# Three of the four inputs of a linear attention are transposed by transfers instead of by TensorE

## The chip, the cores and the metric
The kernel runs on one core of a Trainium2 chip. A core has engines with instruction queues of their own, each executed in order: TensorE (PE, with its weight loads PEld), VectorE (DVE), ScalarE (ACT), GpSimd (POOL) and SyncE (SP), which here only issues transfers. They wait for one another through semaphores. The metric is the device time of one execution in microseconds; three runs of the kernel before had a median of 473.02 us (472.58 to 473.94).

## The reference, cut to what matters
Sizes: 4 batches, 8 heads, 768 steps, head width 48; model width 384, hidden width 1536; all float32 (the weights of the MLP arrive as 64-bit floats).

```
f = sigmoid(f_logit)
for t in range(768):                                   # per batch and head
    state = f[t][:, None] * state + outer(k[t], v[t])  # 48 x 48
    y[t] = q[t] @ state
x = y, heads side by side                              # (4, 768, 384)
out = x + relu(layernorm(x) * g_ln @ w_ch1) @ w_ch2
```

## The kernel before, in words
The 768 steps are cut into twelve units of 64 steps, each with all batches and heads. For each unit n there are the stages of `attention(n)` and then `mlp(n)`, a generator whose `yield`s cut it into pieces.

The attention needs f, q and k with the head width on the partitions. They arrive with the steps on the partitions: a raw tile [128, 2, 8, 64] for each (two batches' 64 steps on the partitions, then two groups g, eight heads of 48 padded to 64). `across` (L607) turns one group with four 128x128 transposes on TensorE (L611) into a PSUM bank, so f, k and q take eight each for a unit. From PSUM, `do_gates` (L641) writes the sigmoids of f into a gate tile on ScalarE; `do_k` and `do_q` multiply k and q by running products of gates (kh, qh; L638, VectorE). The running products are scans on VectorE over a whole unit: `after` (L619) backwards, `upto` (L631) forwards. `kept` is the state multiplied by a unit's total gate. `do_carried` and `do_scores` are 64-row products on TensorE (py L689, ps L703), `do_causal` masks the scores (sc, L707), `do_values` multiplies them by v into py (L729) and copies x out on ScalarE, `do_kt` turns kh (kp L719, copied by L721), `do_chunk` and `do_state` make the next state. Then `normalize` and `turn` make xt (xp L792, scaled by L794), and `sums_of_x` makes sums of its blocks (y, L814).

From the fourth unit on (`FIRST`), the MLP has 15 products by blocks (`by_blocks`, L844, banks bw, bx, by, bz, bv), whose results are copied, added and put through a ReLU into h on ScalarE and VectorE; `sums` (s1 to s4, L823 to L826) on VectorE; then seven products p1, p2, p6, p5, p7, p3, p4 (pp, L935) whose results are added on VectorE and POOL and stored by SP (`put`, L948). PSUM has eight banks: two tiles of two banks (`two_banks`, for py, ps and pn in turn) and four of one bank (`one_bank`), taken in turn by everything else.

The order of every engine's work is written by hand in two strings. START has units 0 to 2 and the loading and unpacking of the weights; UNIT is formatted for each m from 3 to 11, with n = m + 1, o = m + 2, p = m + 3, z = m + 4. A token is one step, issued in this order on the queues of the engines that it uses: `a{n}.stage` a stage, `m{m}` the next piece of the MLP, `l{p}k` a load (four transfers from SP), `s{m}` and `y{n}` the sums, and in START `f`, `r`, `w` for a weight piece, `d` a filler product on TensorE, `t`, `T`, `u`, `U` for sums of weights on VectorE or POOL. Dependencies and buffers then become semaphore waits. A tile with a tag and `bufs=2` has two buffers taken in turn: a third user waits until the first one's readers are done.

Of the kernel before, what the change touches and what calls it, by code (L numbers as in the profile page):

```python
# [8 lines left out]
FP32 = mybir.dt.float32  # L9
I32 = mybir.dt.int32  # L10
U32 = mybir.dt.uint32
AF = mybir.ActivationFunctionType
ALU = mybir.AluOpType
PSUM = bass.MemoryType.PSUM
# [288 lines left out]


START = """
l0k f l0q a0.gates l0x a0.after l0v f r a0.kx a0.upto l1f
d a0.kept a0.k d l1x d d a0.q l1k a0.carried d a0.scores
d a0.causal a0.values w d r a0.kt a0.stats f l1q d a1.gates
f l1v a0.chunk d w a0.norm a1.after a0.state a0.turn d a1.upto a1.kx
a1.k d f r w m0 a1.kept m0 a1.q f f r  # L310
w a1.carried a1.kt r f r l2k f a1.scores a1.causal f l2v
w l2f f a1.values r a1.chunk f a1.stats m0 m0 r w
a1.norm m0 a1.turn r w r w a1.state m0 m1 m1 m1
w m1 w a2.gates r m0 m1 m0 a2.after r l2x w
l2q w a2.kx a2.k a2.upto m1 m0 a2.q m0 m0 l3q l3k
a2.kept l3v m0 a2.carried a2.scores U m1 a2.causal a2.values m1 a2.stats a2.norm
m1 m1 U l3f a2.kt U m1 a2.turn m1 a3.gates T a2.chunk
m2 a3.after a2.state a3.kx l3x l4f m2 a3.k a3.upto a3.kept m2 a3.q
U m2 U l4q a3.carried a3.scores a3.kt U U a3.causal U l4x
a4.gates l4k a3.values T l4v U U a3.chunk m2 a3.stats a3.state t  # L320
l5v U a3.norm m2 s2 a4.after m2 l5f a3.turn m2 m2 a4.kx
a4.k a4.upto l5x l5k m2 U u m2 a4.q m2 y3 l5q
a5.gates a4.kt m2 l6f a4.kept
"""
UNIT = """
m{m} m{m} m{m} a{n}.carried a{o}.after a{n}.scores a{n}.causal m{m} m{m} a{n}.values m{m} m{m}
m{m} m{m} a{n}.stats m{m} m{m} m{m} a{n}.norm m{m} m{m} m{m} s{m} a{n}.chunk
m{m} a{n}.turn m{m} a{o}.upto a{p}.gates a{o}.kx l{p}v a{o}.k a{n}.state m{m} m{m} m{m}
a{o}.kt y{n} m{m} a{o}.q l{p}q l{p}x a{o}.kept l{p}k m{m} l{z}f
"""  # L330


# [1 line left out]
def kernel(  # L334
# [19 lines left out]
    nc = tc.nc  # L354
    B, H, S, D = q.shape
    P = 128
    T = 64
    G = B // 2
    NP = H // 2
    GA = G * NP  # L360
    NS = 2 * GA
    E1 = T + 1
# [4 lines left out]
    NU = S // T  # L367
# [2 lines left out]
    LEAST = 1e-12  # L370
    PLAIN = 2
    FIRST = 3
    PIECE = 768

    outer = ctx.enter_context(tc.tile_pool(name="outer", bufs=1))
# [6 lines left out]
    fast = ExitStack()  # L382
# [2 lines left out]
    raws = fast.enter_context(tc.tile_pool(name="raws", bufs=2))  # L385
    work = fast.enter_context(tc.tile_pool(name="work", bufs=1))
    xs = fast.enter_context(tc.tile_pool(name="xs", bufs=3))
    ps2 = fast.enter_context(tc.tile_pool(name="ps2", bufs=2, space=PSUM))
    ps1 = fast.enter_context(tc.tile_pool(name="ps1", bufs=4, space=PSUM))

    changing = ExitStack()
    stage = changing.enter_context(tc.tile_pool(name="stage", bufs=2))

    def two_banks(name):
        return ps2.tile([P, 2, 512], FP32, tag="two", name=name)

    def one_bank(name):
        return ps1.tile([P, 512], FP32, tag="one", name=name)
# [5 lines left out]
    for name, fill in (("f", 40.0), ("q", 0.0), ("k", 0.0)):  # L404
        t = consts.tile([P, G, H, 64], FP32, name=f"{name}raw")
        nc.gpsimd.memset(t[:, :, :, D:64], fill)
        wide_heads[name] = t
    loaded = {}

    def load(n, name, engines=(nc.sync,)):  # L410
        if n >= NU:
            return
        if name == "x":

            loaded[n, name] = raws.tile([P, G, NP, D], FP32, tag="rawx", name=f"vx{n}")
            odd = v.rearrange("b (a r) s d -> b r s a d", r=2)
            for b in range(B):
                nc.sync.dma_start(out=loaded[n, name][(1 - b % 2) * T:(2 - b % 2) * T, b // 2],
                                  in_=odd[b, 1, n * T:(n + 1) * T])
            return  # L420
        if name == "v":
            vt = raws.tile([P, G, H, D], FP32, tag="rawv", name=f"v{n}")
            loaded[n, name] = vt
        else:
            loaded[n, name] = wide_heads[name]
        src = {"f": f_logit, "k": k, "q": q, "v": v}[name]
        for b in range(B):
            engines[b % len(engines)].dma_start(  # L428
                out=loaded[n, name][(b % 2) * T:(b % 2 + 1) * T, b // 2, :, 0:D],
                in_=src[b, :, n * T:(n + 1) * T, :].rearrange("h p d -> p h d"))  # L430
# [21 lines left out]
    nc.vector.memset(ends[:, :, T:E1], 1.0)  # L452
    starts = consts.tile([P, NS, E1], FP32)
    nc.vector.memset(starts, 0.0)
    gates = []
    for i in range(2):
        t = consts.tile([P, NS * E1 + 1], FP32, name=f"gates{i}")
        nc.gpsimd.memset(t, 0.0)
        gates.append(t)
    least = consts.tile([P, NS], FP32)  # L460
    nc.vector.memset(least, 1.0)
    state = consts.tile([P, 2, GA, D], FP32)
# [66 lines left out]
    mixed = [consts.tile([P, KH, CH], FP32, name=f"mixed{i}") for i in range(1, 5)]  # L529
    to_mix = list(range(0, KH, 2))  # L530

    nothing = consts.tile([P, P], FP32)
    nc.vector.memset(nothing, 0.0)

    def idle():

        nc.tensor.matmul(one_bank("idle")[:, 0:2 * P], lhsT=nothing,
                         rhs=nothing.unsqueeze(1).broadcast_to([P, 2, P]), start=True, stop=True)

    def mix(engine=nc.vector):  # L540
        rows = slice(to_mix[0], to_mix.pop(0) + 2)
# [52 lines left out]

    def attention(n):

        gt = gates[n % 2]
        gv = gt[:, 0:NS * E1].rearrange("p (s e) -> p s e", e=E1)
        HS = NS // G
        flat = "p s e -> p (s e)"  # L600
# [2 lines left out]
        def new(name, shape, **kw):  # L603
            at[name] = work.tile(shape, FP32, tag=name, name=f"{name}{n}", **kw)
            return at[name]
# [35 lines left out]
        def do_gates():  # L641
            new("after", [P, NS, E1])
            new("upto", [P, NS, E1])
            new("total", [P, NS], bufs=2)
            for g in range(G):
                segs = slice(g * HS, (g + 1) * HS)
                pt = across(loaded[n, "f"], g)
                nc.scalar.activation(out=gv[:, segs, 1:E1], in_=pt, func=AF.Sigmoid)  # L648
                if n == 0:
                    scan_after(segs)  # L650
                    scan_upto(segs)
# [7 lines left out]
                scan_upto(slice(0, NS))  # L659

        def do_k_across():
            at["pk"] = [across(loaded[n, "k"], g) for g in range(G)]

        def do_k():
            times(new("kh", [P, NS, T]), at["pk"], at["after"])

        def do_q():
            times(new("qh", [P, NS, T]), [across(loaded[n, "q"], g) for g in range(G)],
                  at["upto"])
            nc.vector.tensor_tensor(out=least, in0=least, in1=at["total"], op=ALU.min)  # L670

        def do_kept():
# [6 lines left out]

        def do_carried():  # L680

            at["py"] = py = two_banks(f"py{n}")
            if not n:
                return
            qh, kept = at["qh"], at["kept"]
            for e in range(GA):
                for b in range(2):
                    for r in range(2):
                        nc.tensor.matmul(py[half(b), r, e * D:(e + 1) * D],  # L689
                                         lhsT=qh[head_rows(r), 2 * e + b],  # L690
                                         rhs=kept[head_rows(r), b, e], start=e == 0, stop=False,
                                         skip_group_check=True)
# [286 lines left out]

    running = {}

    def run(plan):
        for token in plan.split():
            kind, rest = token[0], token[1:]
            if kind == "a":
                n, stage = rest.split(".")
                if int(n) >= NU:
                    continue  # L990
                if "a" + n not in running:
                    running["a" + n] = attention(int(n))
                running["a" + n].pop(stage)()
            elif kind == "m":
                if token not in running:
                    running[token] = mlp(int(rest))
                next(running[token])
            elif kind == "l":
                load(int(rest[:-1]), rest[-1])
            elif kind == "s":  # L1000
                sums(int(rest))
            elif kind == "y":
                if FIRST <= int(rest) < NU:
                    sums_of_x(int(rest))
            else:
                {"r": read, "w": write, "f": fetch, "t": mix, "d": idle,
                 "T": lambda: mix(nc.gpsimd), "u": mix_step,
                 "U": lambda: mix_step(nc.gpsimd)}[token]()
# [2 lines left out]
    assert not (queue or fetched or opened)  # L1011
    for m in range(3, NU):
        run(UNIT.format(m=m, n=m + 1, o=m + 2, p=m + 3, z=m + 4))
        if m == NU - 2:
            worst = consts.tile([P, 1], FP32)
            nc.vector.tensor_reduce(out=worst, in_=least, axis=mybir.AxisListType.X, op=ALU.min)
            pw = one_bank("pw")
            nc.tensor.transpose(pw[0:1, 0:P], worst, ident)
            least_one = consts.tile([1, 1], FP32)
            nc.vector.tensor_reduce(out=least_one, in_=pw[0:1, 0:P], axis=mybir.AxisListType.X,  # L1020
                                    op=ALU.min)
            nc.vector.tensor_scalar(out=small, in0=least_one, scalar1=LEAST, scalar2=None,
                                    op0=ALU.is_lt)
# [37 lines left out]
```

## Time and profile before

| | |
|---|---|
| median of three runs | 473.02 us |
| the profiled execution | 472.82 us, of which the span is 470.7 us |
| TensorE busy | 452.5 us, 96% |
| VectorE, ScalarE, POOL busy | 332.3, 149.7, 93.9 us |
| transfers | 36.32 MB; almost all from SP's queue, whose packets take 36.3% of 16 engines' span |

Busy time is the union of an engine's instructions. TensorE's instructions overlap, so the duration of one is longer than what it adds; what it adds is seen in the spacing of a row of them. The chain that ended last is followed back from the last instruction, at each step to what released it, or to the instruction before it on its engine. Line numbers are those of the kernel before.

### The profile page before, as it was taken

What the parts mean: (1) busy time and instruction counts of PE and PEld (TensorE: products, weight loads), DVE (VectorE), ACT (ScalarE), POOL (GpSimd) and SP (SyncE); (2) the same over time, 40 slices, a digit from 0 to 9 for tenths busy, and PEclk for the clock granted to TensorE, in tenths of its full rate; (3) what the DMA queues carried; (4) which work ended last, traced back from release to release, by engine and by line L of the source; (5) the groups of instructions that cost most, each with busy time, mean ns of one, the idle gap of its engine ahead of it and who ended that gap; (6) DMA issues with size and microseconds to landing.
All of it is one profiled execution on the core that took longest, in us unless ns stands there. A gap on an engine that the chain in (4) does not pass through costs nothing.

```text
span 470.7 us, 13070 instructions
## 1 busy us (share of the span) xinstructions
PE 452.5 (96%) x5655; PEld 420.3 (89%) x5655; DVE 332.3 (71%) x543; ACT 149.7 (32%) x298; POOL 93.9 (20%) x110
## 2 busy tenths in 40 slices
PE   5698999999999999999999999999999999999994
PEld 4487887668899999999999999999999999999994
DVE  6798978236698688578678678677768768666361
ACT  3256652013321341341251242243142241241320
POOL 3215534079222011011011011002002002002010
PEclk9989999999999999999999999999999999999998
DMA  9899980623463302512522522422422410100001
GB/s 167 163 215 239 262 218 2 135 45 65 81 117 78 76 3 55 99 35 52 96 43 52 101 37 50 87 54 43 92 54 42 78 36 9 29 1 18 17 10 33
DMA packets 125969, 36.32 MB, mean 77 GB/s; under 512 B 116432, under 2 KB 122064, under 8 KB 125904
## 3 DMA queue, kind: packets, MB, share of 16 engines
q1 hardware_dynamic: 124128, 35.02, 36.3%
q8 instruction: 46, 0.75, 0.7%
q10 hardware_dynamic: 1776, 0.40, 0.4%
q14 instruction: 19, 0.16, 0.1%
HBM read 30.67 MB, written 4.72 MB: 75 GB/s over the span
## 4 chain that ended last, share of the span: by engine, by line
PE 90%; DVE 3%; SPq 3%; DMA 1%; issue 0%; ACT 0%
PE pp L935 29%; PE bx L844 11%; PE ph L906 9%; PE by L844 9%; PE po L916 7%; PE tr L611 6%; PE bz L844 3%; PE py L729 3%; PE py L689 3%; PE ps L703 2%; PE pn L759 2%; PE kp L719 2%; SPq L428 2%; PE bv L844 2%; PE bw L844 2%; PE xp L792 2%
## 5 line engine op out<-in xcount | busy, mean ns | idle before, releaser
L906 PE MATMUL ph<-xt,w 128*128 128x256 f32 x216 | 48.6, 381 | 0.5 <-DVE kh L638 0.5
L906 PEld LDWEIGHTS ph<-xt,w 128*128 128x128 f32 x216 | 40.4, 190 | 6.5 <-issue 0.9
L935 PE MATMUL pp<-w,h 128*128 128x192 f32 x240 | 42.9, 329 | 0.0
L935 PE MATMUL pp<-mixed,h 128*128 128x192 f32 x240 | 42.3, 326 | 0.0
L935 PE MATMUL pp<-mixed,s 128*128 128x192 f32 x240 | 40.9, 326 | 0.0
L855 ACT ACTIVATE h<-h 128x512 f32<-128x512 f32 x45 | 28.3, 630 | 38.5 <-DVE h L852 37.2
L935 PEld LDWEIGHTS pp<-mixed,h 128*128 128x128 f32 x240 | 39.1, 190 | 0.0
L935 PEld LDWEIGHTS pp<-mixed,s 128*128 128x128 f32 x240 | 38.9, 190 | 0.1
L935 PEld LDWEIGHTS pp<-w,h 128*128 128x128 f32 x240 | 38.6, 190 | 0.4
L747 POOL TENSOR_SCALAR rstd<-mv 128x2 f32<-128x2 f32 x12 | 2.8, 235 | 180.8 <-DVE mv L746 180.7
L852 DVE TENSOR_TENSOR h<-h,by 128x512 f32<-128x512 f32 x36 | 24.8, 688 | 16.9 <-PE by L844 15.9
L619 DVE TENSOR_TENSOR_SCAN after<-gates,ends 128x1040 f32<-128x1040 f32 (+1 forms) x13 | 28.8, 2213 | 5.8 <-ACT gates L648 5.8
L916 PE MATMUL po<-w,h 128*128 128x384 f32 x96 | 32.5, 488 | 0.0
L721 ACT COPY kt<-kp 128x512 f32<-128x512 f32 x24 | 12.9, 591 | 57.5 <-PE kp L719 57.5
L707 DVE TENSOR_TENSOR sc<-ps,causal 128x1024 f32<-128x1024 f32 x12 | 14.7, 1225 | 22.9 <-PE ps L703 22.9
L631 DVE TENSOR_TENSOR_SCAN upto<-gates,starts 128x1040 f32<-128x1040 f32 (+1 forms) x13 | 29.7, 2282 | 0.5
L852 DVE TENSOR_TENSOR h<-h,bx 128x512 f32<-128x512 f32 x27 | 18.3, 679 | 15.9 <-PE bx L844 15.9
L844 PE MATMUL bx<-y,v 128*128 128x128 f32 x216 | 29.4, 279 | 0.0
L736 ACT COPY x<-py 128x384 f32<-128x384 f32 x24 | 10.3, 483 | 59.0 <-PE py L729 59.0
L916 PEld LDWEIGHTS po<-w,h 128*128 128x128 f32 x96 | 17.8, 190 | 10.8
L844 PEld LDWEIGHTS bx<-y,v 128*128 128x128 f32 x216 | 26.2, 192 | 0.7
L943 POOL TENSOR_TENSOR p1x<-p,x 128x192 f32<-128x192 f32 x10 | 10.3, 1032 | 70.9 <-ACT p L950 70.9
(153 smaller groups left out, 940.0 us busy)
## 6 DMA issues: line engine op xcount, KB each, us to landing
w_0words<-in_moe_w_ch_dram SPq DMA_DIRECT2D x7, 768.0 KB, 5.6
kraw<-in_k_dram SPq DMA_DIRECT2D x48, 96.0 KB, 3.4
qraw<-in_q_dram SPq DMA_DIRECT2D x48, 96.0 KB, 3.0
v<-in_v_dram SPq DMA_DIRECT2D x48, 96.0 KB, 3.0
fraw<-in_f_logit_dram SPq DMA_DIRECT2D x46, 96.0 KB, 3.0
vx<-in_v_dram SPq DMA_DIRECT2D x48, 48.0 KB, 2.8
out_dram<-p1x SPq DMA_DIRECT2D x19, 48.0 KB, 2.0
out_dram<-u4y SPq DMA_DIRECT2D x19, 48.0 KB, 2.0
```

What stands on the lines that cost most here:

```text
L611: nc.tensor.transpose(pt[:, a * P:(a + 1) * P], src[:, g, 2 * a:2 * a + 2].rearrange("p h e -> p (h e)"), ident)
L619: nc.vector.tensor_tensor_scan(out=at["after"].rearrange(flat)[:, c0:c1][:, ::-1], data0=gt[:, c0 + 1:c1 + 1][:, ::-1], data1=ends.rearran ...
L631: nc.vector.tensor_tensor_scan(out=at["upto"].rearrange(flat)[:, c0:c1], data0=gt[:, c0:c1], data1=starts.rearrange(flat)[:, c0:c1], initi ...
L689: nc.tensor.matmul(py[half(b), r, e * D:(e + 1) * D], lhsT=qh[head_rows(r), 2 * e + b], rhs=kept[head_rows(r), b, e], start=e == 0, stop=F ...
L707: nc.vector.tensor_tensor(out=new("sc", [P, 2, GA, T]).rearrange("s r e t -> s (r e) t"), in0=at["ps"].rearrange("s r e t -> s (r e) t"), ...
L729: nc.tensor.matmul(py[half(b), r, e * D:(e + 1) * D], lhsT=sc[rows, r, e], rhs=vx[rows, g, a] if r else vt[rows, g, 2 * a], start=n == 0 a ...
L844: nc.tensor.matmul(banks[bank][:, i], lhsT=right[:, i * P:(i + 1) * P], rhs=left, start=new and i == 0, stop=True, skip_group_check=True)
L852: nc.vector.tensor_tensor(out=out[to], in0=out[to], in1=bank, op=op)
L855: nc.scalar.activation(out=out[to], in_=out[to] if bank is None else bank, func=AF.Relu)
L906: nc.tensor.matmul(ph[:, j], lhsT=w1[:, m, (i + j) * P:(i + j + 1) * P], rhs=xt[:, m], start=m == 0, stop=m == KD - 1)
L916: nc.tensor.matmul(po, lhsT=h[:, i, g * P:(g + 1) * P], rhs=w2[:, i], start=i == 0, stop=i == KF - 1)
L935: nc.tensor.matmul(pp, lhsT=a[:, i], rhs=b[:, i], start=i == 0, stop=i == KH - 1)
```

## The change
From unit 5 on (`DIRECT`), f, q and k are no longer transposed on TensorE. ScalarE splits each 32-bit element of a group into its 16-bit halves (`split`, tokens `p{n}{name}{g}`) in a tile `planes` with two buffers; POOL issues a transfer that stores them to DRAM (256 KB); SP issues a transfer that transposes 16-bit elements from DRAM into SBUF (`transfer`, tokens `x{n}{name}`, one transfer for each group). Each half thus makes the way to DRAM and back. The transposed f and q share one tile `turned`, in turn; the transposed k goes to the tile that was q's raw tile, and q's raw data from unit 5 on goes to k's raw tile. The gates are made by one sigmoid over the whole tile, kh and qh by one multiplication each, from SBUF.

There is one gate tile instead of two. py has a PSUM tile of its own (tag `out`), ps and pn share the other. The filler products read the identity instead of a tile of zeros. Each string has a new order; START has five new tokens and otherwise the same ones, among them eleven fillers. The reduction of `least` to `worst` on VectorE comes one unit earlier; the transpose `pw` that reads it stays.

```diff
+    DIRECT = 5
-    ps2 = fast.enter_context(tc.tile_pool(name="ps2", bufs=2, space=PSUM))
+    ps2 = fast.enter_context(tc.tile_pool(name="ps2", bufs=1, space=PSUM))
-    def two_banks(name):
-        return ps2.tile([P, 2, 512], FP32, tag="two", name=name)
+    def two_banks(name, tag="two"):
+        return ps2.tile([P, 2, 512], FP32, tag=tag, name=name)
+    turned = {}
+    drams = fast.enter_context(tc.tile_pool(name="drams", bufs=2, space=bass.MemoryType.DRAM))
+    halved = {}
+    def raw_of(n, name):
+        return wide_heads["k" if n >= DIRECT and name == "q" else name]
+    def split(n, name, g):
+        if n >= NU or n < DIRECT:
+            return
+        if (n, name) not in halved:
+            halved[n, name] = drams.tile([G, P, 2, 64 * H], U16, tag=f"{name}halves",
+                                         name=f"{name}halves{n}")
+        planes = raws.tile([P, 2, 64 * H], U16, tag="planes", name=f"{name}planes{n}_{g}")
+        nc.scalar.copy(
+            out=planes.rearrange("p two c -> p c two"),
+            in_=raw_of(n, name)[:, g].rearrange("p h e -> p (h e)").bitcast(U16).rearrange(
+                "p (c two) -> p c two", two=2))
+        nc.gpsimd.dma_start(out=halved[n, name][g], in_=planes)
+    def transfer(n, name):
+        if n >= NU or n < DIRECT:
+            return
+        if not turned:
+            turned["k"] = wide_heads["q"].rearrange("p g h e -> p (g h e)").rearrange(
+                "p (s t) -> p s t", t=T)
+            turned["f"] = turned["q"] = late["pool"].tile([P, NS, T], FP32, name="turned")
+        there = halved.pop((n, name))
+        for g in range(G):
+            to = turned[name].rearrange("p (g s) t -> p g (s t)", g=G)[:, g].bitcast(U16)
+            nc.sync.dma_start_transpose(out=to.rearrange("p (a r) -> p a r", a=NP),
+                                        in_=there[g].rearrange("p two c -> (p two) c"))
-    gates = []
-    for i in range(2):
-        t = consts.tile([P, NS * E1 + 1], FP32, name=f"gates{i}")
+    gates = consts.tile([P, NS * E1 + 1], FP32)
...
+            if n >= DIRECT:
+                nc.scalar.activation(out=gv[:, :, 1:E1], in_=turned["f"], func=AF.Sigmoid)
+                return
...
+                nc.vector.tensor_tensor(out=kh, in0=turned["k"], in1=at["after"][:, :, 1:E1],
+                                        op=ALU.mult)
...
+                nc.vector.tensor_tensor(out=qh, in0=turned["q"], in1=at["upto"][:, :, 1:E1],
+                                        op=ALU.mult)
...
-            at["py"] = py = two_banks(f"py{n}")
+            at["py"] = py = two_banks(f"py{n}", "out")
...
-        if m == NU - 2:
+        if m == NU - 3:
             worst = consts.tile([P, 1], FP32)
             nc.vector.tensor_reduce(out=worst, in_=least, axis=mybir.AxisListType.X, op=ALU.min)
+        if m == NU - 2:
             pw = one_bank("pw")
```

UNIT before and after:

```
m{m} m{m} m{m} a{n}.carried a{o}.after a{n}.scores a{n}.causal m{m} m{m} a{n}.values m{m} m{m}
m{m} m{m} a{n}.stats m{m} m{m} m{m} a{n}.norm m{m} m{m} m{m} s{m} a{n}.chunk
m{m} a{n}.turn m{m} a{o}.upto a{p}.gates a{o}.kx l{p}v a{o}.k a{n}.state m{m} m{m} m{m}
a{o}.kt y{n} m{m} a{o}.q l{p}q l{p}x a{o}.kept l{p}k m{m} l{z}f

a{o}.after m{m} m{m} a{n}.carried a{n}.scores p{o}q0 m{m} a{n}.causal m{m} m{m} m{m} p{o}q1
l{p}k m{m} a{n}.values a{o}.upto a{n}.chunk a{n}.stats m{m} x{o}q p{p}f0 m{m} m{m} m{m}
m{m} m{m} x{o}k m{m} m{m} p{p}k0 p{p}k1 a{n}.norm s{m} m{m} l{p}x m{m}
a{o}.q p{p}f1 l{p}q x{p}f m{m} a{n}.turn a{o}.k m{m} m{m} y{n} l{p}v m{m}
a{p}.gates l{z}f a{n}.state m{m} a{o}.kept a{o}.kt
```

The last three lines of START after (the transfers of unit 5's f and the first of the other splits):

```
a3.stats m2 a4.kx U a3.norm s2 m2 p5f0 a3.state l5k m2 a4.k
U m2 p5f1 m2 a4.kt u a3.turn l6f x5f p5k0 a4.upto a4.q
l4x p5k1 y3 l5q a5.gates m2 m2 l5x a4.kept m2
```

## The prediction, made before the changed kernel was run
> **What bounds the kernel now.** I read the page's busy shares first, then its 40 slices, the chain that ended last, and the chain in order of time through one steady unit.
>
> ```profile
> span 470.7 us, 13070 instructions
> PE 452.5 (96%) x5655; PEld 420.3 (89%) x5655; DVE 332.3 (71%) x543; ACT 149.7 (32%) x298; POOL 93.9 (20%) x110
> PE   5698999999999999999999999999999999999994
> PE 90%; DVE 3%; SPq 3%; DMA 1%; issue 0%; ACT 0%
> ```
>
> TensorE is busy nearly all the time; only the first three slices and the last have room. A busy share alone does not prove that work on TensorE sets the end, so the chain comes next:
>
> ```profile
> 315.32 2.15 PE pp L935 x12
> 317.46 0.66 PE xp L792 x6
> 318.12 1.95 PE pp L935 x12
> 320.07 1.75 PE tr L611 x16
> 321.82 5.85 PE pp L935 x36
> 327.67 0.87 PE kp L719 x8
> 328.55 1.95 PE pp L935 x12
> 330.50 0.87 PE tr L611 x8
> ```
>
> From 43.76 us to 436.31 us this chain is TensorE following itself, with no gap. A unit runs from 299.87 (its py L689 product) to 336.00: 36.13 us. So a TensorE instruction taken away is worth its spacing, as long as nothing else becomes late. The other engines have room per unit:
>
> ```profile
> 318.00:354.00 36.00, 36.00 (x498) 35.19 (x497) 26.58 (x48) 11.09 (x24) 3.59 (x6) 1.00 0.32 62
> ```
>
> Columns: stretch, its length, busy us of PE, PEld, DVE, ACT, POOL, granted clock, DMA share, GB/s. The clock is 1.00.
>
> **What is removed.** For n from 5 to 11, seven units lose three groups of eight transposes (f, k, q). A group is worth 0.87 to 0.875 us (16 take 1.75). 21 x 0.875 = 18.4 us. The same line in the table of groups says 273 ns for one transpose, but that is latency: they overlap, and 168 x 0.273 = 45.9 would be wrong. The Trainium skill ("TensorE: Matmul & The Clock Gate", Part 4) gives about 390 ns alone and 275 ns in one kernel; the second agrees with the duration, and either as a price would promise 46 to 66 us. The spacing decides.
>
> The check of the smallest gate waits for DVE before its transpose at 436.83, 0.5 us of TensorE idle; its reduction now stands a unit earlier, so 0.5 us goes.
>
> **What is added, unit by unit.** I lay out a new steady unit from its bw product, t = 0, with the durations of the chain above and its neighbours (0.89 a block product, 1.95 a pp product, carried 1.08, scores 0.95, values 1.08, chunk 1.08, xp 0.66, kp 0.87, and some 0.2 after each 64-row group). The last block product ends at 18.0; p1 and p2 at 19.9 and 21.9; p6 23.8; xp 24.5; p5, p7, p3, p4 26.4, 28.4, 30.3, 32.3; kp 33.2; the unit ends at 36.13 - 2.62 = 33.5.
>
> ScalarE: six splits of 1024 elements. Rows:
>
> ```profile
> L504 ACT ACTIVATE w_0upper<-w_0words 128x768 f32<-128x768 f32 x7 | 6.5, 927 | 7.7 <-DMA w_0words<-in_moe_w_ch_dram 5.2 <-POOL w L520 2.5
> L769 ACT COPY state<-pn 128x768 f32<-128x768 f32 x1 | 0.8, 799 | 0.5 <-PE pn L759 0.5
> ```
>
> 768 elements with a stride of two take 0.93, dense 0.80; by length 1024 take 1.07 to 1.24; I take 1.23, the strided row. 6 x 1.23 = 7.4 on top of 11.1, so 18.5 of 33.5: room. Two sigmoids of 0.60 become one of 1024, 1.07 to 1.24 likewise: nothing gained. VectorE: kh and qh were 2 x 2 x 0.68 = 2.7; two of 1024, by L826 (768 in 1.23) up to 1.6 each, by L707 (1024 in 1.23) 1.23 each; I take 1.25, so 26.4 of 33.5, hidden. POOL gets six DMA issues: 0 to 1.9 us each (its largest add, L520), I take 0.63, what SP needs for one; at most 11.4 + 3.6 of 33.5, hidden in sum. SP: six transposing issues, four loads as before; SP's own queue waits for VectorE before its stores (in all 87.5, 34.9 and 12.3 us in its three commonest waits), so it has room. DMA share is 0.32; the stores and transfers add 768 rows of 2 KB and some 6 x 1024 of 256 B against some 9,700 packets a unit now (16 loads of 512 rows, four of 256, eight stores of 64), so about 0.6 at the packet time of now (36.3% of 16 x 470.7 over 124128: 22 ns).
>
> None of this lies on TensorE's path in sum. What counts is latency, and two waits are new:
>
> (a) a{p}.gates on ScalarE waits for f's transfer; queued behind it are the two kt copies and the copies of bw and bx. bv takes the bank that kt's first copy empties. bv starts in the next unit at 33.5 + 0.89 + 0.89 + 1.08 + 0.95 = 37.3; the kt copy is 0.59, so gates must end by 36.7. On VectorE, after (2.39) waits for gates, with the causal mask and h's adds behind it, but values comes only at 42.
>
> (b) the planes have two buffers, so the split of f's second half waits until k's first half has been stored, and behind that split xt's scalings wait.
>
> Two sums lead to gates. By SP: xn and s's sums end at 24.2 on VectorE, p1x at 24.5, its two stores issue (1.16), four q loads (2.72), to 28.4; then both f transfers, L; then gates 1.2. By planes: last block product 18.0 + subtract 0.69 + relu 0.63 = 19.3, split 20.5, store S, split 1.23, store S, one transfer t, gates 1.2: 22.9 + 2S + t.
>
> Nothing in the trace is a store of this size or a transfer that transposes. Rows:
>
> ```profile
> w_0words<-in_moe_w_ch_dram SPq DMA_DIRECT2D x7, 768.0 KB, 5.6
> kraw<-in_k_dram SPq DMA_DIRECT2D x48, 96.0 KB, 3.4
> out_dram<-p1x SPq DMA_DIRECT2D x19, 48.0 KB, 2.0
> ```
>
> S: 2.0 for 48 KB is below, 5.6 for 768 KB plus a 1.9 issue, 7.5, above; between them by size 256 KB lands in 3.0, with a 0.63 issue 3.7, which I take. t: 2.0 below; above, if it went out as pieces of 32 B (16 rows of 2 B), 8192 pieces x 22 ns / 16 = 11.3. Nearest are the loads: two 512-packet loads have the 1024 packets of one half's rows, 0.63 + 3.4 = 4.0; I take that. For the pair, four loads: 3 x 0.63 + 3.4 = 5.3; lower 2.6, upper 22.5.
>
> Then gates ends by SP at 28.4 + 5.3 + 1.2 = 34.9, by planes at 22.9 + 7.4 + 4.0 = 34.3. Both are under 36.7, by 1.8 and 2.4 us. q: its second split ends near 10.3, stored by 14.0, pair landed 19.3, needed at 24.5. k follows on the same queue: 24.6 against 26 for its multiply. So f is tight, q and k are not.
>
> A rule against this: the Trainium skill ("GPSIMD Engine Reference", Key points) says POOL shares its SBUF interfaces with VectorE and contends when VectorE has two SBUF inputs. The trace agrees: POOL's add of p1 and x takes 0.98 beside s's sums at 317.95, and 0.59 at 325.64. Two of f's and k's stores are issued at that point, so with 0.4 more each the planes sum would be 35.1, still in time. And "VectorE: DVE Perf Modes" (The three transpose paths) gives 1.3 us for a 128x128 by transfer; 16 in a row make a pair of 21 us, estimated, while "DMA: Bandwidth & Descriptors" (Latency and other measured facts) has 261 GB/s, a pair of 2 us plus fixed cost. No run shows either yet.
>
> **The order at the start.** The eleven fillers of TensorE stay eleven, two of them now after the first products of the MLP (up to 0.9 us); q is loaded sooner, the first weight piece 4 x 0.63 = 2.5 later, but VectorE gets to it only at 16.7, 5.9 after it landed (10.83). From 22.64 to 36.9 VectorE is contiguous in the old chain, with the same instructions in the new order. I take +0.9 and bounds of -2 (the 1.35 us wait at 41.68 filled, and a little) and +2.5. Unit 5's first transfers have 14 us until bv: hidden.
>
> **Sum.** 472.8 (the profiled execution: span 470.7 and 2.1 around it) - 18.4 - 0.5 + 0.9 = 454.8; the median of the runs shown lies 0.2 above: 455.
>
> **Rivals.**
> 1. f comes late by up to 3 us a unit (L 7.1 to 10, or 2S + t 13.8 to 17). The six units m = 3 to 8 each pay e, the lateness. Price 6e: 455 to 473. For it: three unknown terms, margins of two us. Against: the nearest rows.
> 2. The other side: the same wait beyond its point, e over 3.15 (18.9 / 6), L over 10.2 or S over 6.5 at t = 4. Place: ScalarE before gates, kt behind it, TensorE before bv. At L = 13, 6 x 5.9 = 35: 490. For it: the 32-byte bound.
> 3. Transfers are limited by 32-byte pieces: three pairs of 22.5 a unit on one queue, 67 us where 33.5 are: over 500, up to 455 + 6.5 x 34 = 676. For it: nothing shows the opposite; against: it needs every piece priced as a packet.
> 4. The transposes were not on the path, 472 to 474: excluded almost, since the chain has them back to back.
>
> **How the numbers follow.** Chances: the forecast 0.60 (own range 451 to 460: -2 and +2.5 of the start, up to 0.4 us a unit more), rival 1 0.13, rival 2 0.15, rival 3 0.10, rival 4 0.02. Faster: 0.60 and 0.11 of rival 1, 0.71; within 0.3% (what a measurement of this kernel can tell) 0.03; slower 0.26. The range goes from 450 to 487, leaving out rival 3, part of rival 2 and the tip below.
>
> **What would show it.** Right: the groups tr with 120 transposes instead of 288; units of 33.5 us; no gap before bv; transfers of f landing within 7 us of issue; the sigmoid of f ended before kp's copies are wanted. Wrong: idle time of ScalarE before gates ended by a transfer, with TensorE idle before bv or bw; splits waiting for a store; SP waiting for stores. If a pair lands in over 10 us, the forecast has the wrong sign.

## The result and the profile after

The changed kernel takes 560.67 us (median; 556.05 to 561.87), the kernel before 473.29 in runs beside it: a ratio of 1.183, 95% interval 1.176 to 1.190. It is 18% slower where I had forecast 4% faster, and it lies far outside my range of 450 to 487.

The page of the kernel after: the span, the busy time of the engines, TensorE and its granted clock in 40 slices, the chain that ended last, and the first three groups of the table of groups.

```profile
span 560.2 us, 13028 instructions
PE 475.0 (85%) x5487; PEld 434.6 (78%) x5487; DVE 326.9 (58%) x528; ACT 335.5 (60%) x333; POOL 116.7 (21%) x151
PE   5699999999886799769686976988697698999995
PEclk9799999999899879779977978997797889999998
PE 37%; issue 24%; ACT 16%; DMA 9%; SPq 4%; DVE 4%; POOL 3%; POOLq 0%; ACTq 0%; DVEq 0%
L432 ACT COPY qplanes<-kraw 128x1024 uint16<-128x1024 uint16 x14 | 66.8, 4770 | 0.0
L432 ACT COPY fplanes<-fraw 128x1024 uint16<-128x1024 uint16 x14 | 66.3, 4775 | 0.0
L432 ACT COPY kplanes<-kraw 128x1024 uint16<-128x1024 uint16 x14 | 65.2, 4916 | 0.0
```

The transposes did leave TensorE: 5487 products instead of 5655, the 168 that I counted. But from the eleventh slice on, where unit 5's first splits stand, its row has holes, its clock drops to 0.7 in places, and it carries 37% of the chain instead of 90%. The three groups at the head of the table are the splits: 42 of 4.8 us, 198 us of ScalarE. I had taken 1.23 us for one.

The new transfers are not to blame. Stores and transposing transfers, in the list of DMA issues of the same execution (destination and source, issuing queue, count, KB where known, median us from issue to landing):

```profile
fhalves<-fplanes POOLq DMA_DIRECT2D x14, 256.0 KB, 3.4
khalves<-kplanes POOLq DMA_DIRECT2D x14, 256.0 KB, 2.3
qhalves<-qplanes POOLq DMA_DIRECT2D x14, 256.0 KB, 2.9
turned<-fhalves SPq DMA_TRANSPOSE x14, 3.8
turned<-qhalves SPq DMA_TRANSPOSE x14, 4.0
qraw<-khalves SPq DMA_TRANSPOSE x14, 4.2
```

These are close to what I had worked out from the loads. What a slow split does is seen in ScalarE's timeline of a steady unit (start, duration, operation, idle time before it; "..." marks lines left out):

```profile
312.51 0.60 ACT L898 ACTIVATE h<-bx 128x512 f32<-128x512 f32 x1 [0.30 <-PE bx L893]
313.01 4.76 ACT L432 COPY qplanes<-kraw 128x1024 uint16<-128x1024 uint16 x1
317.26 0.93 ACT L898 ACTIVATE h<-bv 128x512 f32<-128x512 f32 x1
319.74 0.63 ACT L904 ACTIVATE h<-h 128x512 f32<-128x512 f32 x1 [1.54 <-DVE h L901]
320.27 4.76 ACT L432 COPY qplanes<-kraw 128x1024 uint16<-128x1024 uint16 x1
...
337.62 9.29 ACT L432 COPY kplanes<-kraw 128x1024 uint16<-128x1024 uint16 x2
346.43 0.65 ACT L999 COPY p<-pp 128x192 f32<-128x192 f32 x1
346.98 4.75 ACT L432 COPY fplanes<-fraw 128x1024 uint16<-128x1024 uint16 x1
351.24 1.82 ACT L843 ACTIVATE xt<-xp,gain 128x128 f32<-128x128 f32 x6
```

ScalarE has hardly a pause. bv was ready at 315.6 and is copied at 317.3; p1 is copied behind two splits in a row. And TensorE waits for these copies. Its waits, seen at the weight loads, between 160 and 490 us (who waits, for whom: us in all, times, longest):

```profile
PEld xp L841 <- ACT p L999: 28.2, 6, 4.9
PEld bz L893 <- ACT h L898: 16.2, 6, 2.9
PEld bx L893 <- ACT h L898: 13.5, 7, 1.9
PEld by L893 <- DVE h L901: 7.7, 14, 1.7
PEld pp L984 <- DVE p1x L992: 7.2, 6, 1.3
```

Not one of them is the wait that I had feared most, bv for kt's copy behind gates. A unit takes 48.7 us (bw at 310.69 and at 359.42) where I had 33.5.

### The profile page after: what moved, and what is told of

The parts are those of the page before. It is cut to its first block, busy times and chain, and to the rows that moved or that the text cites. A ratio compares the mean times of both kernels' runs of the same rounds, so it can differ in the third digit from the quotient of the medians.

```text
span 560.2 us, 13028 instructions
## 1 busy us (share of the span) xinstructions
PE 475.0 (85%) x5487; PEld 434.6 (78%) x5487; DVE 326.9 (58%) x528; ACT 335.5 (60%) x333; POOL 116.7 (21%) x151
## 4 chain that ended last, share of the span: by engine, by line
PE 37%; issue 24%; ACT 16%; DMA 9%; SPq 4%; DVE 4%; POOL 3%; POOLq 0%; ACTq 0%; DVEq 0%
PE pp L984 14%; ACT qplanes L432 9%; PE ph L955 7%; PE po L965 4%; PE bx L893 3%; DMA w_0words<-in_moe_w_ch_dram 3%; ACT fplanes L432 2%; SPq L470 2%; PE by L893 2%; ACT kplanes L432 2%; DVE h L901 1%; DMA fhalves<-fplanes 1%; DMA w_512words<-in_moe_w_ch_dram 1%; PE kp L768 1%; DMA fraw<-in_f_logit_dram 1%
## 5 line engine op out<-in xcount | busy, mean ns | idle before, releaser
L432 ACT COPY qplanes<-kraw 128x1024 uint16<-128x1024 uint16 x14 | 66.8, 4770 | 0.0
L432 ACT COPY fplanes<-fraw 128x1024 uint16<-128x1024 uint16 x14 | 66.3, 4775 | 0.0
L432 ACT COPY kplanes<-kraw 128x1024 uint16<-128x1024 uint16 x14 | 65.2, 4916 | 0.0
L984 PE MATMUL pp<-mixed,s 128*128 128x192 f32 x240 | 53.7, 387 | 4.8 <-DVE p1x L992 4.8
L984 PEld LDWEIGHTS pp<-mixed,s 128*128 128x128 f32 x240 | 49.5, 232 | 7.2 <-DVE p1x L992 7.2
L955 PE MATMUL ph<-xt,w 128*128 128x256 f32 x216 | 48.7, 381 | 1.0 <-ACT xt L843 1.0
L841 PE MATMUL xp<-ident,xn 128*128 128x128 f32 x72 | 13.5, 315 | 28.1 <-ACT p L999 26.7
L436 POOL DMA_DIRECT2D qhalves<-qplanes x14 | 7.7, 547 | 128.1 <-ACT qplanes L432 128.1
L893 PE MATMUL bx<-y,v 128*128 128x128 f32 x216 | 34.3, 310 | 0.0
L841 PEld LDWEIGHTS xp<-ident,xn 128*128 128x128 f32 x72 | 9.4, 157 | 30.1 <-ACT p L999 28.2
L655 DVE TENSOR_TENSOR_SCAN after<-gates,ends 128x1040 f32<-128x1040 f32 (+1 forms) x13 | 28.7, 2207 | 6.5 <-ACT gates L687 3.5
L893 PEld LDWEIGHTS bx<-y,v 128*128 128x128 f32 x216 | 31.2, 223 | 0.5
```

Of the source, the lines that this page charges most:

```text
L432: nc.scalar.copy(out=planes.rearrange("p two c -> p c two"), in_=raw_of(n, name)[:, g].rearrange("p h e -> p (h e)").bitcast(U16).rearrang ...
L436: nc.gpsimd.dma_start(out=halved[n, name][g], in_=planes)
L655: nc.vector.tensor_tensor_scan(out=at["after"].rearrange(flat)[:, c0:c1][:, ::-1], data0=gt[:, c0 + 1:c1 + 1][:, ::-1], data1=ends.rearran ...
L841: nc.tensor.transpose(pt[:, m], xn[:, g, m * P:(m + 1) * P], ident)
L893: nc.tensor.matmul(banks[bank][:, i], lhsT=right[:, i * P:(i + 1) * P], rhs=left, start=new and i == 0, stop=True, skip_group_check=True)
L955: nc.tensor.matmul(ph[:, j], lhsT=w1[:, m, (i + j) * P:(i + j + 1) * P], rhs=xt[:, m], start=m == 0, stop=m == KD - 1)
```

## The experiments

My theory, A: a split is slow because it writes 16-bit elements in turn to two places 1 KB apart, and this alone makes the loss. Rivals: B, copies of 16-bit integers are slow on ScalarE in any order; C, the transfers cost the time and the splits lie beside them; D, the new order is itself a loss.

### The same split, walked plane by plane

```diff
-            out=planes.rearrange("p two c -> p c two"),
+            out=planes,
             in_=raw_of(n, name)[:, g].rearrange("p h e -> p (h e)").bitcast(U16).rearrange(
-                "p (c two) -> p c two", two=2))
+                "p (c two) -> p two c", two=2))
```

> Same split, same data, but walked plane by plane: consecutive 2-byte writes and reads every 4 bytes, where the changed kernel reads consecutively and writes to two places 1 KB apart in turn. Theory A (the alternating writes cost the 4.77 us): a split takes 1.1 to 1.3 us like the 32-bit rows of before (1024 elements at 1.04 to 1.21 ns), ScalarE loses 42 x 3.5 = 147 us of busy time, and the time falls to 453 to 463 us. Theory B (16-bit integer copies are slow on ScalarE whatever their order): splits stay near 4.8 us and the time near 560. Theory C (the transfers or stores are the cause, splits only lie beside it): splits get short and the time stays over 500.

Measured: 451.83 us, a ratio to before of 0.951 (0.948 to 0.955). The page, one line of the splits (ns: least, median, most), and a stretch of the chain in order of time:

```profile
PE 432.7 (96%) x5487; PEld 402.2 (89%) x5487; DVE 329.0 (73%) x528; ACT 185.9 (41%) x333; POOL 121.3 (27%) x151
L432 ACT COPY qplanes<-kraw x14: 1029/1034/1066, 155.8 to 362.1; 128x1024 uint16<-128x1024 uint16 x14
```

```profile
319.78 0.89 PE bw L893 x8
320.68 0.89 PE bx L893 x8
321.57 1.08 PE py L738 x64
322.65 0.95 PE ps L752 x64
323.59 1.09 PE bv L893 x8
```

A split takes 1.03 us, the chain is TensorE without a gap again, and a unit is 33.2 us (py at 321.57 and 354.80). B and C fall: the elements, the transfers and all dependencies are the same. (A further kernel meant for B, with a plain consecutive copy in place of the split, gave no time; the consecutive copy among the forms below stands in for it.) Two words in an access pattern are worth 109 us, and this kernel beats both others. It lands 3 us under my forecast for the change.

### The new order alone

All units are transposed on TensorE; k's load moves behind k's multiplication, which makes its own transposes. The start's order loads unit 6's f ahead of unit 5's gates, so that in this kernel unit 5 has gates from unit 6's f; nothing is left out.

```diff
-    DIRECT = 5
+    DIRECT = NU
-l{p}k m{m} a{n}.values ...
+m{m} a{n}.values ...
-... a{n}.turn a{o}.k m{m} ...
+... a{n}.turn a{o}.k l{p}k m{m} ...
```

> The new order, one gate tile and the new PSUM tags, without any transfer: all units are transposed on TensorE, k's two groups at its multiplication, and k's load moved behind it. If the new order costs nothing by itself: 471 to 476. If the order (its start, or PSUM tags) has part in the loss: over 480. At most the start shows the 2.7 us by which the changed kernel's first pp product is later (137.4 against 134.7).

Measured: 470.68 us, 0.993 of before (0.991 to 0.996). D falls: the order, with the one gate tile and the new PSUM tags, gains some 3 us. The step from here to the plane-by-plane kernel is 470.68 - 451.83 = 18.9 us, against the 18.4 that I had for the 168 transposes.

### What each tensor's splits cost

One of the three names keeps the changed kernel's walk (14 splits, 7.5 us more of ScalarE in a unit), the other two go plane by plane. For f:

```diff
+        if name in "f":
+            nc.scalar.copy(out=planes.rearrange("p two c -> p c two"),
+                           in_=raw16.rearrange("p (c two) -> p c two", two=2))
+        else:
+            nc.scalar.copy(out=planes, in_=raw16.rearrange("p (c two) -> p two c", two=2))
```

> The plane-by-plane split for k and q, the changed kernel's walk for f alone: 14 splits of 4.77 us instead of 1.04, 7.5 us more of ScalarE in a unit. If the loss goes with ScalarE's busy time: a third of 109, 488. If free time of ScalarE in the unit (about 15 of 33.5 us) takes it up except where something waits: under 488, 455 to 478; the first split stands before the copy of bz, the second before xt's scalings, and f's halves come 2 x 3.7 us later against a margin of 1.8, so not under 455.

> The same for q alone. With busy time: 488. By place: the first split stands before the copy of bv, the second before the ReLU and the copy of x; q has 5 us of margin, so the loss is what these copies hold up, 1 to 4 us a unit in six to seven units: 458 to 480.

> The same for k alone. With busy time: 488. By place: the two splits stand in a row before the copy of p1, so POOL's and VectorE's p1x come 7.4 us later, and with them q's loads, f's transfers and the bank of p1: 3 to 6 us a unit, 470 to 495, more than f or q.

| slow splits | time, us | more than 451.8 | ScalarE busy, % | TensorE's largest waits at the weight loads, 160 to 460 us |
|---|---|---|---|---|
| f | 483.38 | 31.6 | 49 | bz for ScalarE's h: 14.1 us |
| q | 480.51 | 28.7 | 49 | bx for ScalarE's h, by for VectorE's h: 11.6 us each |
| k | 503.31 | 51.5 | 47 | xp for the copy of p1: 29.1 us |
| all (the changed kernel) | 560.67 | 108.9 | 60 | these four, and pp for p1x: above |

The three add up to 111.8, about the whole. Both my readings were off. A third for each (488) fails for k. That free time would take most of it up fails too: ScalarE is busy half of the time, and yet f and q lose about 30 us each, 4 to 5 us a unit. What counts is what stands right behind a split, and the waits of each kernel are at that place. k's two stand in a row before the copy of p1, and I had put k at the most, but too low (470 to 495).

### Load on ScalarE, with the halves in time

The plane-by-plane split, and behind each a second, slow copy that nobody reads:

```diff
+        spare = raws.tile([P, 2, 400], U16, tag="spare", bufs=1, name=f"spare{name}{n}_{g}")
+        nc.scalar.copy(
+            out=spare.rearrange("p two c -> p c two"),
+            in_=w2[:, 0:2].rearrange("p i c -> p (i c)").bitcast(U16)[:, 0:800].rearrange(
+                "p (c two) -> p c two", two=2))
```

> Plane-by-plane split, and behind each a second copy of 800 elements in the changed kernel's walk, from a weight tile to a spare tile that nobody reads, some 3.7 us. ScalarE is as loaded as in the changed kernel and at the same places, but the halves leave 3.7 us sooner. Theory 1 (the loss is what waits on ScalarE's queue behind a split: copies of products, ReLUs, xt's scalings): 540 to 565, as the changed kernel. Theory 2 (the loss is f, q and k that come late because their halves are stored late): 452 to 470.

Measured: 555.46 us, 1.167 of before (1.163 to 1.171). TensorE's waits, at the weight loads, between 160 and 490 us:

```profile
PEld xp L846 <- ACT p L1004: 28.9, 6, 4.9
PEld bz L898 <- ACT h L903: 15.7, 6, 2.9
PEld bx L898 <- ACT h L903: 13.6, 7, 2.0
PEld by L898 <- DVE h L906: 8.0, 14, 1.7
PEld pp L989 <- DVE p1x L997: 3.3, 6, 0.6
```

The first four are the waits of the changed kernel to within a microsecond, although the halves left 3.7 us sooner; the fifth is 3.3 where it was 7.2. So the loss is the work that stands behind a split on ScalarE's queue, and the banks that TensorE gets back late. That q and k themselves come late can account for little: the times differ by 5 us, by their ratios to before 7.5 us, and the spare copies are 0.1 us longer than what they replace (1.03 and 3.84 against 4.77), 4 us in all. For f this kernel is no such test: its transfers stand on SP's queue behind the stores of p1x, which the splits delay in both kernels, so that its sigmoid starts hardly sooner in the unit (1.3 us before the bw at 207.94, in the changed kernel 0.6 before the one at 208.85). For f the list has to do: no product waits for gates or for the kt copies behind it.

### How much margin the transfers have

The plane-by-plane kernel issues f's two transfers twice.

```diff
-        for g in range(G):
+        for g in [0, 1, 0, 1] if name == "f" else range(G):
```

> Plane-by-plane split, and f's two transfers issued twice, same data to the same place, so f's second landing is later by two issues of 1.23 us, 2.5 us. The prediction's margin for gates was 1.8 us before TensorE waits at bv; the plane-by-plane run shows kt's first copy end at 321.7 and bv start at 323.5, also 1.8. If that margin is the real one: 0.7 us late in each of six units, 4 us, 455 to 458 where the plane-by-plane kernel has 451.8. If something else gives way sooner (VectorE's scan behind gates): over 460. If the margin is larger: 451 to 453.

Measured: 478.36 us, 1.004 of before (1.0003 to 1.008), by the ratios some 25 us more than with one pair. That is far over the 455 to 458 of my margin, and it falls among "over 460", though not for the reason given there: VectorE's scan does wait 33.8 us for gates in all, but TensorE waits for VectorE only 0.5 us in the stretch below. Its wait is the one that I had named first, seen at the weight loads between 190 and 380 us, in an execution of 481.54 us:

```profile
PEld bv L893 <- ACT kt L770: 14.2, 5, 3.3
```

The delay was larger than meant, in part because the second pass over a half writes where the first one writes and so waits for its landing: SP waits 11.0 us for landings of f in seven units, the longest 2.9, and the plane-by-plane kernel has no such wait. SP's queue and ScalarE's timeline show the transfers' issue and the sigmoid that ends their wait, first plane by plane with one pair, then with two:

```profile
347.79 2.63 SPq L449 DMA_TRANSPOSE turned<-fhalves  x2
352.74 1.06 ACT L682 ACTIVATE gates<-turned 128x1024 f32<-128x1024 f32 x1 [7.01 <-DMA turned<-fhalves]
```

```profile
258.85 6.63 SPq L449 DMA_TRANSPOSE turned<-fhalves  x4
269.27 1.06 ACT L682 ACTIVATE gates<-turned 128x1024 f32<-128x1024 f32 x1 [11.94 <-DMA turned<-fhalves]
```

From the first issue to the sigmoid: 4.95 and 10.42, 5.5 us later and not 2.5. TensorE then stood up to 3.3 us before bv, which agrees with a margin of about 2. Part of the rest is the clock: behind such a stop the eight products of bv took 2.08 us instead of 1.16, and over whole executions 0.963 to 0.978 was granted instead of 0.990 to 0.995. So the margin of 1.8 us is not contradicted, but the experiment, with a delay over twice as large as meant, does not measure it.

### What makes the walk slow

Two kernels have groups of four copies behind the last unit of the plane-by-plane kernel, with little beside them.

```diff
+        nc.scalar.copy(out=fa, in_=src16)                                          # consecutive
+        nc.scalar.copy(out=pa.rearrange("p two c -> p c two"), in_=...)            # in turn, 1 KB apart
+        nc.scalar.copy(out=fa.rearrange("p (b two e) -> p b e two", two=2, e=8), in_=...)  # 16 bytes
+        nc.scalar.copy(out=fa.rearrange("p (c two) -> p c two", two=2), in_=...)   # reads in turn
...
+            nc.scalar.copy(out=fa.rearrange("p (two c r) -> p c two r", two=2, r=r), in_=...)  # runs
```

> The kernel with the plane-by-plane split, and behind its last unit ten kinds of copies, four of each, nothing else beside them; only their durations count (the time grows by their sum). On ScalarE, 1024 elements of 16 bits: consecutive to consecutive; the changed kernel's walk (writes in turn 1 KB apart); writes in turn 16 bytes apart; reads in turn 1 KB apart, writes consecutive; the plane-by-plane walk; 512 elements written every 4 bytes; and 512 elements of 32 bits written in turn 1 KB apart, and consecutively. On VectorE the two walks of the split. Theory A1 (each write to another place than the one before costs, whatever the distance): 4.8 us for 1 KB and for 16 bytes, 1.0 to 1.1 for reads in turn, 32 bits in turn 2.2 to 2.5. Theory A2 (only far jumps cost): 1.1 for 16 bytes apart. Theory A3 (16-bit writes that don't follow one another cost, because part of a word is written): 32 bits in turn 0.6 to 0.7 as consecutive, 512 written every 4 bytes 2.2 to 2.5. VectorE: slow too if it is the memory, about 1.1 if it is ScalarE's own.

> The kernel with the plane-by-plane split, and behind its last unit seven kinds of ScalarE copies, four of each, for their durations. 1024 elements of 16 bits written in turn to two places 1 KB apart in runs of 2, 4, 8 and 32 elements before the change of place; then to four places 512 bytes apart, one element each; then 512 elements written every 4 bytes to one row (again); then 1024 written one element every 16 bytes. If each change of place costs (3.6 ns at runs of one): runs of 2, 4, 8, 32 take 2.9, 2.0, 1.5, 1.2. If only a write of part of a 4-byte word costs: runs of 2 already take 1.05 to 1.1. Every 16 bytes: 4.7 if any jump costs, 1.5 if a steady step is cheap as the step of 4 bytes was.

The table of groups by form, of the first of the two (mean ns of one is the second number behind the bar):

```profile
L1085 ACT COPY pa<-kraw 128x1024 uint16<-128x1024 uint16 x4 | 4.2, 1046 | 12.3 <-DMA out_dram<-u4x 12.3
L1087 ACT COPY pa<-kraw 128x1024 uint16<-128x1024 uint16 x4 | 19.1, 4783 | 0.1
L1089 ACT COPY pa<-kraw 128x1024 uint16<-128x1024 uint16 x4 | 18.9, 4723 | 0.1
L1091 ACT COPY pa<-kraw 128x1024 uint16<-128x1024 uint16 x4 | 4.6, 1156 | 0.1
L1093 ACT COPY pa<-kraw 128x1024 uint16<-128x1024 uint16 x4 | 4.2, 1044 | 0.1
L1095 ACT COPY pa<-kraw 128x512 uint16<-128x512 uint16 x4 | 3.0, 760 | 0.1
L1097 ACT COPY pa<-kraw 128x512 f32<-128x512 f32 x4 | 4.3, 1072 | 0.1
L1099 ACT COPY pa<-kraw 128x512 f32<-128x512 f32 x4 | 2.5, 618 | 0.1
L1101 DVE COPY pb<-kraw 128x1024 uint16<-128x1024 uint16 x4 | 11.0, 2742 | 0.1
L1103 DVE COPY pb<-kraw 128x1024 uint16<-128x1024 uint16 x4 | 2.8, 695 | 0.1
```

In order: consecutive 1.05; in turn 1 KB apart 4.78; in turn 16 bytes apart 4.72; reads in turn 1.16; plane by plane 1.04; 512 written every 4 bytes 0.76; 32-bit elements in turn 1.07 for 512, consecutive 0.62; VectorE's two walks 2.74 and 0.69. So it is the writes, not the reads, and 16 bytes cost as much as 1 KB; 32-bit writes in turn pay less; VectorE pays too. For the second kernel, from the lines of the instructions (ns: least, median, most):

```profile
L1086 ACT COPY pa<-kraw x16: 1044/1044/1080, 446.2 to 462.5; 128x1024 uint16<-128x1024 uint16 x16
L1093 ACT COPY pa<-kraw x4: 4736/4737/4737, 463.6 to 477.9; 128x1024 uint16<-128x1024 uint16 x4
L1096 ACT COPY pa<-kraw x4: 617/617/618, 482.6 to 484.6; 128x512 uint16<-128x512 uint16 x4
L1098 ACT COPY pa<-kraw x4: 4715/4715/4715, 485.2 to 499.5; 128x1024 uint16<-128x1024 uint16 x4
```

Runs of 2, 4, 8 and 32 elements all take 1.04: two neighbours, 4 bytes, before each change of place already make it cheap (L1086). Four places in turn cost as much as two (L1093), a steady step of 16 bytes as much as jumps (L1098). The 512 elements of L1096 were meant to be written every 4 bytes again, but the pattern, `fa.rearrange("p (two c) -> p c two", two=2)[:, :, 0]`, is the first half of the row, consecutive; so its 0.62 is the price of 512 consecutive writes, and the step of 4 bytes (L1095 of the first kernel: 0.76) costs a quarter more. "Each change of place costs" falls, since runs of two still change place 512 times. "A write of part of a 4-byte word costs" doesn't hold as it stands either, since the step of 4 bytes is cheap. What fits them all is that a lone 16-bit write costs 4.6 ns if neither of its neighbours in time falls near it; where "near" ends, between 4 and 16 bytes of step, was not tried, and why a lone 32-bit write costs less than half of that (1.07 us for 512, 2.1 ns) was not shown.

## Why the prediction was wrong, point by point

The step that failed is one term: "768 elements with a stride of two take 0.93, dense 0.80; by length 1024 take 1.07 to 1.24; I take 1.23". It measured 4.77, and 4.77 / 1.23 is a factor of 3.9. The row that I scaled by length, the unpacking of the weights, *reads* with a stride and writes consecutively. The split wrote with a stride, back and forth, and in 16 bits. No row of the trace had that, so both ends of my bound came from rows of another kind. I had bounded stores and transfers from both sides over a factor of about four and more, because they were visibly new; the split looked familiar. With 4.77 the same working gives 6 x 4.77 + 11.1 = 39.7 us of ScalarE in a unit of 33.5, so it would have shown a new bound.

- *TensorE is the path, a group is worth 0.875 us.* Right: 18.9 us between the order alone and the plane-by-plane kernel, 18.4 forecast; units of 33.2, 33.5 forecast.
- *Stores S = 3.7, transfers t = 4.0.* Right: 0.55 to issue and 2.3 to 3.4 to land; 3.8 to 4.2. An issue of a transfer takes SP 1.23 and not 0.63.
- *gates ends 34.9 after bw, 1.8 before bv would wait.* Right in the plane-by-plane kernel: the sigmoid ends at 321.18, 34.6 after its unit's bw (319.78 less a unit), and kt's first copy 1.8 us before bv; over the steady units 33.9 to 35.0, and 1.5 to 2.6 before bv.
- *DMA share about 0.6.* Too low: 0.77 to 0.88 in the full steady units of the plane-by-plane kernel. The packets came out as counted (some 6,800 more a unit, 6,900 reckoned), so the added ones took longer than the 22 ns of before: some 34, an estimate from 0.79 x 33 - 0.32 x 36 = 14.6 us of 16 engines a unit. No wait of TensorE came of it.
- *None of the added work lies on TensorE's path in sum.* Wrong by the same term, and in a second way: with one name slow, ScalarE was busy for 57 to 66 of the 100 us between 200 and 300, and it cost 29 to 52 us, because the queue is in order. I had looked at what stands behind the waiting instruction (gates), and not behind a long one.
- *The start and the order: +0.9, -0.5.* Together +0.4, with my bounds -2.5 to +2. The order alone measured -3.1, and that is nearly all by which the plane-by-plane kernel lies under the forecast of 455. What of it came from the start and what from the units was not separated.
- *The rivals.* The loss had none of their mechanisms. Their place, bv behind gates, shows up only when f's transfers are doubled, and for 1.0 us in one unit with f's splits slow. "Below 10.2 us a pair the change gains" could not be seen, as the splits decided.
- *The rules weighed.* The contention of POOL with VectorE and the 1.3 us a block were not what mattered: POOL's issues took 0.54 to 0.75, and a half of eight blocks landed in 3.4 to 5.6.

The rule that spoke against this change was one that I did not look for. The Trainium skill ("SBUF — State Buffer", Door 1: The DMA port swizzle) says that SBUF has lines of 16 bytes, that each access to a new line pays, and that two hits in a line are enough to hide it. The copies agree: runs of two and steps of 4 bytes cheap, 16 bytes and 1 KB alike slow; only the reads hardly paid (1.16 against 1.05). It gives no price; the runs show 4.6 ns for a lone 16-bit write and 2.1 ns for a 32-bit one.

## What to carry to other kernels

Before scaling a row by length, compare the whole access pattern, and the writes first: a copy whose successive 16-bit writes lie 16 bytes or more apart cost four and a half times as much here (4.72 against 1.05), and changing the places of its two loops was enough to avoid it. A new instruction on an in-order queue must be checked for what stands behind it and for the banks that this frees, not only for the engine's busy share. And the least familiar part (here the transfers) is not the one to bound alone; every added instruction without a row of its own kind deserves both ends.

## What the runs showed of the hardware that I had not expected

Stops of TensorE cost more than their length. The changed kernel has TensorE busy for 475.0 us, the plane-by-plane kernel with the same products 432.7: 42 of the 109 us lie in its busy time, with a mean granted clock of 0.918 against 0.991. The ratio of the clocks alone would make it 432.7 x 0.991 / 0.918 = 467 us, an estimate, so some 34 of the 42. Beside the waits of some 2 to 5 us in each unit, the clock is 0.85 to 0.92 in the stretches from 175 to 485 us, where the kernel before and the plane-by-plane kernel have 1.00 in their steady units. The longer the stops, the lower it is here: with only f or q slow, where the longest are 2.4 and 2.1 us, stretches of 35 us between 175 and 420 us have 0.95 to 1.00, and with only k slow, where they are 4.9 us, 0.85 to 0.96.

Transposing transfers were no slower than the 4.0 us that I had worked out from two loads with as many rows: 256 KB of f or q landed in 3.4 to 5.6 us in the plane-by-plane kernel, median 3.9, and three pairs a unit ran beside everything else without any wait of TensorE for them.
